# Attention, routing and two feed-forward layers on one core: scores by bank, casts placed around GpSimd, squares moved to the expert stage

## The chip, the cores and the metric

The kernel runs on one core of a Trainium2 chip. TensorE (PE) multiplies, VectorE (DVE), ScalarE (ACT) and GpSimd (POOL) work on elements, SyncE (SP) and queues of the other engines start transfers. The metric is the time of the device for one launch, the median of three runs; lower is better.

## The reference

Four batches of eight heads with 576 rows of 64 go through a causal attention with a decay; its output is a table of 2304 tokens of 512. Each token is routed to one of eight experts by the cosine with the experts' embeddings, and scaled by its gate. A second layer, common to all tokens, follows.

```python
scores = scale * np.matmul(q, k.transpose(0, 1, 3, 2))
decay = cum[:, :, :, None] - cum[:, :, None, :]          # cum: running sum of log f
scores = np.where(causal, -1e9, scores + decay)          # softmax over the last axis, times v
xn = x / (norm(x) + 1e-06);  en = expert_emb / (norm(expert_emb) + 1e-06)
logits = xn @ en.T / tau;    expert_idx = argmax(logits) # gate_w: softmax's value there
out[mask] = gate_w[mask, None] * (np.maximum(x[mask] @ w1[e], 0) @ w2[e])      # for each e
h = np.maximum(np.maximum(x @ w1, x @ w2), x @ w3);  return h @ w_out
```

The norm of a token scales all its logits alike, so the choice of the expert doesn't need it; the gate does. The sums of squares of the tokens' rows are therefore wanted late, when the gates are worked out.

## The kernel before

Attention runs over 32 heads in 16 pairs. A head's 576 rows are five blocks t of 64, 128, 128, 128 and 128 rows that see 64, 192, 320, 448 and 576 columns. Products are made from numbers split in a high part and a rest: for each pair `split_tasks` casts q to `At` (`q_hi`) and k to `R1` (`k_hi`), on VectorE or ScalarE, and GpSimd subtracts to get the rests (`q_lo`, L321, and `k_lo`, L324). `q_lo` reads q and its cast, `k_lo` reads k and its cast. In the trace casts and evictions stand on L433 (VectorE) or L435 (ScalarE), the lines of the helper `evict`.

A score tile is one bank of `ps_s` (three banks): `s_task` writes it with two products, `At` by `R` over 128 rows and `Bt` by `R` over 66 (L344), no narrower than 192 columns. Block t = 4 takes two tiles of 288 columns, so a head has six tiles, in the order t = 4, 0, 3, 1, 2. `r_task` reduces each on VectorE (L361: scale, mask and row minimum in one instruction, written to `P`, and a read of the accumulator to `nm`), which frees the bank; ScalarE's exponential follows (L381). `P` is turned by transposes on TensorE into banks of `ps_t` (two named t, L397 and L401, one named tl for the last 64 columns of each block, L393 and L399), which are evicted to `PT`. `pair_out` multiplies with v (`po`, L459), evicts to `ot`, turns back with the logits beside it (`pb`, L478), divides by the sums (L445, L446) and writes `XL` (L487) and x to memory.

After the last pair of a batch `batch_out` starts two chains: `route_batch`, which ranks the batch's tokens by expert and adds them to a table of rows (VectorE steps and a few products), and `square_sums`, five ScalarE squares (L703). Batch 3's routing is followed by the gathers for the experts.

The expert stage computes for each of eight experts, with 384 to 256 tokens, eight tiles `ph` and from them `h`, then four tiles `py` into `Y`; weights come through the ring `stg` on SP's queue and are cast to `w` (L934) with a subtraction behind; tokens come through gathers, a transpose (`xt`) and a cast to `x` (L934). The part of `Y` beyond the first expert's columns is cleared once (L1103). `side_work` works out norms and gates beside it. The shared layer follows from about 500 us.

All of this is put in order by a list scheduler, `Sched`: a task has engines with costs, a priority and predecessors, and the plan takes at each step the task that can start first, of these the one with the lowest priority number. The instructions are issued in the plan's order on each engine; a predecessor that only the plan knows makes no wait on the chip. There an instruction waits for the data, buffers and registers that it uses and for those ahead of it on its engine.

Of the kernel before, what the change touches and what calls it, by code (L numbers as in the profile page):

```python
# [12 lines left out]
ALU = mybir.AluOpType  # L13
# [201 lines left out]
def attention(tc, g, qT, kT, v, x_dram, es):  # L215
# [132 lines left out]

    def r_task(h, t, k, j0, w, n, ext):
        def fn(e):  # L350
            if k == 0:
                if t == order[0] and h % H == 0:
                    b = h // H
# [6 lines left out]
            m0 = S - 128 if t == 0 else S - ext + j0  # L360
            nc.vector.tensor_tensor_reduce(out=P[0:n, j0:j0 + w], in0=st_.pop((h, t, k))[0:n, 0:w], in1=g.mask[0:n, m0:m0 + w],  # L361
                                           scale=-0.125, scalar=(3.0e38 if k == 0 else nm[0:n, 0:1]),
                                           op0=ALU.add, op1=ALU.min, accum_out=nm[0:n, k:k + 1])

        deps = [fs[h, t, k]] + ([fr[h, t]] if k else [])
        fr[h, t] = sd.task("DVE", dve(w), fn, slot[h, t], deps, get=None if k else ("P", (h, t)), rel=[("s", (h, t, k))])

    def head(h):
        p, r = divmod(h, 2)
        b = h // H  # L370
        T = PT[h % NPT]
# [14 lines left out]
        for t in order:  # L386
# [20 lines left out]
            if t == 0:  # L407
                continue
# [1051 lines left out]
```

## Time and profile before

| what | us |
|---|---|
| median of three runs | 785.85 (785.13 to 787.29) |
| the profiled execution | 785.06 |
| its span, first to last instruction | 783.3 |
| TensorE busy | 738.9 (94%) |
| VectorE, ScalarE, GpSimd busy | 461.9, 368.2, 237.7 |

The profile is of one execution. Its stages, by the trace: attention from about 15 to 222 us, the routing of batch 3 with the first gathers to 238, experts to about 500, the shared layer to the end. A line of a group names engine, operation, output and inputs with their sizes and the number of instructions. A timeline's line gives the start, the duration and, in brackets, how long the engine had nothing to do and what it waited for. Matmuls overlap: from one start to the next is what one costs.

### The profile page before, as it was taken

How to read it: one execution, taken by the hardware profiler on the slowest of the kernel's cores; microseconds unless marked ns; L12 is line 12 of the kernel's file. 1: busy time of each engine (PE TensorE's matmuls, PEld its weight loads, DVE VectorE, ACT ScalarE, POOL GpSimd, SP SyncE). 2: the span in 40 equal slices, each digit the busy share in tenths (PEclk: the TensorE clock that was granted, in tenths of full speed). 3: DMA queues.
4: the chain of work that ended last, by engine and by line, in shares of the span. 5: the costliest groups of instructions: out<-in, count | busy, mean ns of one | idle time of the engine just before them, and what ended most of it. 6: DMA issues, size and time to landing. Idle time of an engine off the chain costs nothing.

```text
span 783.3 us, 13403 instructions
## 1 busy us (share of the span) xinstructions
PE 738.9 (94%) x4862; PEld 682.3 (87%) x4862; DVE 461.9 (59%) x1076; ACT 368.2 (47%) x870; POOL 237.7 (30%) x189
## 2 busy tenths in 40 slices
PE   2989999999949998999999999999999999999996
PEld 1868877778738998999999999989999899999995
DVE  6888887988567998867767877941211211112110
ACT  5668887978836653454554563231211212212111
POOL 7464443532020344234223113341221211212112
PEclk9999999999978999999999999999999999999998
DMA  9959775751145465556474653200000000100001
GB/s 228 239 125 216 191 178 143 182 118 40 23 116 208 151 220 181 186 181 233 151 257 147 230 198 126 82 28 14 1 40 1 28 14 1 41 0 15 28 1 43
DMA packets 44614, 90.19 MB, mean 115 GB/s; under 512 B 23320, under 2 KB 23320, under 8 KB 44544
## 3 DMA queue, kind: packets, MB, share of 16 engines
q1 hardware_dynamic: 40960, 77.83, 34.0%
q0 software_dynamic: 3152, 9.88, 3.5%
q10 hardware_dynamic: 432, 1.57, 0.5%
q8 instruction: 40, 0.66, 0.3%
q14 instruction: 30, 0.25, 0.1%
HBM read 74.97 MB, written 9.44 MB: 108 GB/s over the span
## 4 chain that ended last, share of the span: by engine, by line
PE 75%; DVE 9%; DMA 7%; issue 4%; ACT 1%; POOL 1%; SPq 1%; POOLq 0%; DVEq 0%; ACTq 0%
PE pm L907 10%; PE pm L906 10%; PE pm L908 10%; PE s L344 6%; PE po L459 6%; PE t L397 4%; PE ph L908 3%; PE ph L907 3%; PE py L906 3%; PE py L908 3%; PE ph L906 3%; PE py L907 3%; PE po L1268 3%; PE po L1267 3%; PE po L1266 3%
## 5 line engine op out<-in xcount | busy, mean ns | idle before, releaser
L1240 DVE TENSOR_TENSOR tm<-pm,tm 128x384 f32<-128x384 f32 x72 | 40.1, 557 | 199.4 <-PE pm L908 198.2
L907 PE MATMUL pm<-x_y,m 128*128 128x384 f32 x432 | 144.5, 335 | 0.0
L908 PE MATMUL pm<-x_y,m 128*128 128x384 f32 x432 | 144.4, 334 | 0.0
L906 PE MATMUL pm<-x_y,m 128*128 128x384 f32 x432 | 144.4, 334 | 0.0
L381 ACT ACTIVATE P<-P,nm 128x576 f32<-128x576 f32 (+4 forms) x160 | 88.3, 555 | 17.0 <-DVE nm L361 16.7
L344 PE MATMUL s<-R,At 128*128 128x192 f32 (+1 forms) x192 | 71.3, 380 | 14.9 <-DVE At L271 10.5
L934 ACT ACTIVATE w<-stg 128x1024 fp32r<-128x1024 f32 x63 | 66.2, 1056 | 33.3 <-DMA stg<-in_w_dram 14.4
L907 PEld LDWEIGHTS pm<-x_y,m 128*128 128x128 f32 x432 | 81.1, 188 | 0.6 <-POOL x_y L1199 0.3
L951 DVE TENSOR_TENSOR w<-stg,w 128x1024 fp32r<-128x1024 f32 x54 | 70.2, 1304 | 19.3 <-ACT w L934 18.9
L907 PE MATMUL ph<-x,w 128*128 128x384 f32 (+7 forms) x256 | 79.3, 310 | 2.1 <-DVE x L1083 2.1
L906 PEld LDWEIGHTS pm<-x_y,m 128*128 128x128 f32 x432 | 81.1, 188 | 0.2
L908 PEld LDWEIGHTS pm<-x_y,m 128*128 128x128 f32 x432 | 81.1, 188 | 0.0
L906 PE MATMUL py<-h,w 128*128 128x384 f32 (+7 forms) x256 | 79.5, 311 | 0.8 <-DVE h L1141 0.8
L908 PE MATMUL ph<-x,w 128*128 128x384 f32 (+7 forms) x256 | 79.4, 310 | 0.8 <-DVE w L951 0.7
L906 PE MATMUL ph<-x,w 128*128 128x384 f32 (+7 forms) x256 | 79.4, 310 | 0.7 <-ACT x L934 0.7
L1251 POOL TENSOR_TENSOR g<-tm,g 128x384 fp32r<-128x384 f32 x34 | 36.5, 1074 | 141.4 <-ACT g L934 141.4
L908 PE MATMUL py<-h,w 128*128 128x384 f32 (+7 forms) x256 | 78.5, 307 | 0.4 <-DVE w L951 0.4
L907 PE MATMUL py<-h,w 128*128 128x384 f32 (+7 forms) x256 | 78.2, 305 | 0.0
L934 ACT ACTIVATE g<-tm 128x384 fp32r<-128x384 f32 x36 | 18.8, 524 | 115.9 <-DVE tm L1240 115.9
L361 DVE CUSTOM_DVE_ANT_0 P<-s,mask 128x288 f32<-128x288 f32 (+4 forms) x160 | 64.4, 422 | 11.1 <-PE s L344 6.7
L344 PE MATMUL s<-R,Bt 66*128 66x192 f32 (+1 forms) x192 | 60.2, 320 | 4.3 <-DMA R<-clo 4.3
L321 POOL TENSOR_TENSOR At<-q,At 64x1152 fp32r<-64x1152 f32 x15 | 40.3, 2684 | 77.1 <-DVE At L433 24.7
(246 smaller groups left out, 1620.4 us busy)
## 6 DMA issues: line engine op xcount, KB each, us to landing
stg<-in_w_dram SPq DMA_DIRECT2D x61, 512.0 KB
q<-in_q_dram SPq DMA_DIRECT2D x32, 288.0 KB
k<-in_k_dram SPq DMA_DIRECT2D x32, 288.0 KB
sd<-in_m_dram SPq DMA_DIRECT2D x18, 512.0 KB
Bt<-At SPq DMA_DIRECT2D x16, 288.0 KB
v<-in_v_dram SPq DMA_DIRECT2D x4, 1024.0 KB
x_dram<-XL SPq DMA_DIRECT2D x64, 64.0 KB
sd_o<-in_mo_dram SPq DMA_DIRECT2D x6, 512.0 KB
```

Of the source, the lines that this page charges most:

```text
L321: nc.gpsimd.tensor_tensor(out=At[i][64:128], in0=raws[p][0][64:128], in1=At[i][64:128].bitcast(F32), op=ALU.subtract)
L344: nc.tensor.matmul(st[:, 0:wp], lt[0:kk, r, ROW0[t]:ROW0[t] + 128], rt[0:kk, r, j0:j0 + wp], start=(ps_i == 0), stop=(ps_i == 1))
L361: nc.vector.tensor_tensor_reduce(out=P[0:n, j0:j0 + w], in0=st_.pop((h, t, k))[0:n, 0:w], in1=g.mask[0:n, m0:m0 + w], scale=-0.125, scalar ...
L381: nc.scalar.activation(out=P[0:n, 0:ext], in_=P[0:n, 0:ext], func=AF.Exp, bias=nm[0:n, k:k + 1], scale=-1.0, accum_out=sums[b][0:n, t, h % ...
L459: nc.tensor.matmul(po[64 * r:64 * r + 64, lo - c0:w], vt[b][0:n, a, (2 * hp + r) * D:(2 * hp + r + 1) * D], PT[(2 * p + r) % NPT][0:n, a, ...
L906: nc.tensor.matmul(out, whi, xhi, start=start, stop=False)
L907: nc.tensor.matmul(out, whi, xlo, start=False, stop=False)
L908: nc.tensor.matmul(out, wlo, xhi, start=False, stop=stop)
L934: nc.scalar.activation(out=out, in_=in_, func=AF.Copy)
L951: ENG[e].tensor_tensor(out=w[:, 1], in0=t, in1=w[:, 0].bitcast(F32), op=ALU.subtract)
L1240: nc.vector.tensor_tensor(out=mx[0], in0=mx["p", w][:, 0:MC], in1=mx[0], op=ALU.max)
L1251: ENG[e].tensor_tensor(out=ht[:, 1, :], in0=mx[0], in1=ht[:, 0, :].bitcast(F32), op=ALU.subtract)
```

## The change

Casts. The costs in the plan become 1.1 (ScalarE) and 0.8 us (VectorE), 2.7 us for a subtraction. Both casts of a pair get the pair before's `k_lo` as a predecessor, `q_lo` gets both casts and `k_lo` gets `q_lo`. The instructions and what they read are the same.

```diff
-        qh = sd.task(("ACT", "DVE"), (1.02, 0.67), q_hi, u, old + [load])
-        ql = sd.task("Pool", 2.6, q_lo, u, [qh])
+        qh = sd.task(("ACT", "DVE"), (1.1, 0.8), q_hi, u, old + [load, quiet[0]])
         qc = sd.task("SP", 0.9, q_copy, u, [qh], lat=2.0)
-        kh = sd.task(("ACT", "DVE"), (1.02, 0.67), k_hi, u, old + [load])
-        kl = sd.task("Pool", 2.6, k_lo, u, [kh])
+        kh = sd.task(("ACT", "DVE"), (1.1, 0.8), k_hi, u, old + [load, quiet[0]])
+        ql = sd.task("Pool", 2.7, q_lo, u, [qh, kh])
+        kl = quiet[0] = sd.task("Pool", 2.7, k_lo, u, [kh, ql])
```

Scores. Six tiles of a head become four units, one bank each: the halves of t = 4, t = 2 with t = 1, and t = 3 with t = 0, whose product is now 64 columns wide. The reductions of a shared bank go in the reverse order, and the last one frees it.

```diff
+    UNITS = (((4, 0, 0, 288, 0),), ((4, 1, 288, 288, 0),), ((2, 0, 0, 320, 0), (1, 0, 0, 192, 320)), ((3, 0, 0, 448, 0), (0, 0, 0, 64, 448)))
+    FLIPS = ((4,), (2, 1), (3, 0))
...
+    def s_unit(h, n):
...
+        u = slot(h, n)
+
+        def mm(e):
+            st = st_[h, n] = ps_s.tile([128, 512], F32, tag="s", name=f"s_{h}_{n}")
+            for t, k, j0, w, c in UNITS[n]:
+                for ps_i, (lt, rt, kk) in enumerate(((At[i], R1[i], 128), (Bt[i], R2[i], 66))):
+                    nc.tensor.matmul(st[:, c:c + w], lt[0:kk, r, ROW0[t]:ROW0[t] + 128], rt[0:kk, r, j0:j0 + w],
+                                     start=(ps_i == 0), stop=(ps_i == 1))
+
+        cost = 0.08 + sum(2 * max(0.112, 0.013 + x[3] / 2400) for x in UNITS[n])
+        dep = fs[h, n] = sd.task("PE", cost, mm, u - LEAD, ready[p], get=("s", (h, n)))
+        for x, (t, k, j0, w, c) in enumerate(UNITS[n][::-1]):
+            def red(e, t=t, k=k, j0=j0, w=w, c=c):
+                if n == 0 and h % H == 0:
                     sums[b] = sm.tile([128, NBLK, H], F32, tag="sums", name=f"sums{b}", bufs=2)
                     nc.vector.memset(sums[b][64:128, 0, :], 1.0)
-                P = pp.tile([128, S], F32, tag="P", name=f"P_{h}_{t}")
-                nm = sm.tile([128, 2], F32, tag="nm", name=f"nm_{h}_{t}")
-                Pt[h, t] = P, nm
-            P, nm = Pt[h, t]
...
+                if k == 0:
...
+                nc.vector.tensor_tensor_reduce(out=P[0:m, j0:j0 + w], in0=st_[h, n][0:m, c:c + w], in1=g.mask[0:m, m0:m0 + w],
+                                               scale=-0.125, scalar=(3.0e38 if k == 0 else nm[0:m, 0:1]),
+                                               op0=ALU.add, op1=ALU.min, accum_out=nm[0:m, k:k + 1])
...
+            end = x == len(UNITS[n]) - 1
+            dep = fr[h, t] = sd.task("DVE", dve(w), red, u, [dep] + ([fr[h, t]] if k else []), get=None if k else ("P", (h, t)),
+                                     rel=[("s", (h, n))] if end else [])
...
+                fe[h, t] = sd.task("ACT", 0.28 + EXT[t] / 1200, exp, u, [fr[h, t]])
+
+    def slot(h, n):
+        return 5 * h + (0, 0.5, 1.5, 3)[n]
```

Transposes. Three groups t = 4, t = 2 with 1, and t = 3 with 0 take the place of four; the tl bank is taken at a head's start.

```diff
+        def tail(t, P):
+            nc.tensor.transpose(tl_[h][0:64, 128 * t - 128:128 * t], P[:, 128 * t:128 * t + 64], g.ident)
+
+        def start(e):
+            tl_[h] = ps_t.tile([128, 512], F32, tag="tl", name=f"tl_{h}", bufs=1)
+            tail(4, Pt[h, 4][0])
...
+        u4 = slot(h, 0) + LT
+        ft[h, "tl"] = sd.task("PE", 0.06, start, u4, [fe[h, 4]], get=("tl", h))
...
+            def tr(e, ts=ts):
+                w = tl_[h, ts] = ps_t.tile([128, 512], F32, tag="t", name=f"t_{h}_{ts[0]}")
+                c = 0
+                for t in ts:
+                    P = Pt.pop((h, t))[0]
+                    for a in range(t):
+                        nc.tensor.transpose(w[:, c:c + 128], P[:, 128 * a:128 * a + 128], g.ident)
+                        c += 128
+                    if t == 0:
+                        nc.tensor.transpose(w[0:64, c:c + 64], P[0:64, 0:64], g.ident[0:64, 0:64])
+                    elif t != 4:
+                        tail(t, P)
+
...
+            ft[h, n] = sd.task("PE", cost, tr, u + LT, [fe[h, t] for t in ts] + [ft[h, "tl"]], get=("t", (h, n)),
+                               rel=[("P", (h, t)) for t in ts])
...
-        fv[h, 0] = sd.task(("ACT", "DVE"), (act(256), dve(256)), tail, slot[h, order[-1]] + LT - 4,
-                           [ft[h, t] for t in order] + old, rel=[("tl", h)])
+        fv[h, "tl"] = sd.task(("ACT", "DVE"), (act(256), dve(256)), corners, slot(h, 3) + LT - 4,
+                              [ft[h, n] for n in range(len(FLIPS))] + old, rel=[("tl", h)])
```

Routing and squares. Batches 0 to 2 only reduce their logits when they end; one routing handles fifteen blocks after batch 2. The squares of these batches leave attention. In the expert stage, SP reads x again into the unused part of `Y`, ScalarE squares it there, and only then is that part cleared; `side_work` comes after these squares.

```diff
-        sd.chain(g.square_sums(b, lambda: XL[b][:, :, :, 0:D]), pr + 40, deps + [consts_done])
+        if b == B - 1:
+            sd.chain(g.square_sums(b, lambda: XL[b][:, :, :, 0:D]), pr + 40, deps + [consts_done])
...
+def logits(nc, g, b, lg):
+    yield dict(eng="DVE", cost=0.75)
+    nc.vector.tensor_reduce(out=g.L[:, NBLK * b:NBLK * b + NBLK, :], in_=lg().rearrange("p t h c -> p t c h"), op=ALU.add, axis=AX.X)
...
+def route_batch(nc, g, b, lg, rp, sp, ps):
+    yield from logits(nc, g, b, lg)
+    if b < B - 2:
+        return
...
+    m, b0 = (1, b) if last else (B - 1, 0)
+    s0, nb = NBLK * b0, NBLK * m
...
+    for c in range(m):
+        yield dict(eng="DVE", cost=0.83)
+        ohp = onehot_pos(nc, g, rm[:, NBLK * c:NBLK * c + NBLK], NBLK, keep, "rb")
+        yield dict(eng="PE", cost=0.2, get=None if c else ("o", ("pt", b)))
+        if c == 0:
+            pt = ps.tile([128, 512], F32, tag="o", name=f"ptab{b}")
+        table_sums(nc, pt, ohp, rr[:, NBLK * c:NBLK * c + NBLK], c == 0, c == m - 1)
+    yield dict(eng="DVE", cost=0.24, rel=[("o", ("pt", b))])
+    table_add(nc, g, pt)
```

```diff
-    sd.chain(side_work(nc, g, g.cp, rp, ps_o), 30.0, [sorted_])
...
-    zero = [sd.task("ACT", 1.8, lambda e, d=d: clear(e, d), now + 16, [wsplit[1, 0, 3]]) for d in range(KC)]
+    room = [Y[d][:, CAP[0]:CAP[0] + 4 * DM].rearrange("p (t d) -> p t d", t=4) for d in range(KC)]
+    xv = x_dram.rearrange("(b n) d -> b n d", n=S)
+
+    def fetch(e, d):
+        if d < B - 1:
+            nc.sync.dma_start(out=room[d], in_=xv[d, 64:S].rearrange("(t p) d -> p t d", p=128))
+        else:
+            nc.sync.dma_start(out=room[d][0:64, 0:B - 1], in_=xv[0:B - 1, 0:64].rearrange("b p d -> p b d"))
+
+    def square(e, d, i):
+        n, col = (128, NBLK * d + 1 + i) if d < B - 1 else (64, NBLK * i)
+        x = room[d][0:n, i]
+        nc.scalar.activation(out=x, in_=x, func=AF.Square, accum_out=g.ss[0:n, col:col + 1])
+
+    zero, norms = [], []
+    for d in range(KC):
+        xl = sd.task("SP", 1.5, lambda e, d=d: fetch(e, d), now + 10 + 5 * d, [wsplit[1, 0, 3]], lat=4.0)
+        mine = [sd.task("ACT", 0.62, lambda e, d=d, i=i: square(e, d, i), now + 18 + 6 * d, [xl]) for i in range(4 if d < B - 1 else B - 1)]
+        zero.append(sd.task("ACT", 1.8, lambda e, d=d: clear(e, d), now + 18 + 6 * d, mine))
+        norms += mine
+    sd.chain(side_work(nc, g, g.cp, rp, ps_o), 50.0, [sorted_] + norms)
```

How the order moves. First VectorE, at the casts of pair 10 (`q_10`, `k_10`): `P` with `nm` is a reduction of a score tile `s_`, named by the block in its first number (before) or by the unit (now), and `ot` an eviction. Before:

```order
L433 CAST At_111<-q_10_1514 128x1152
L361 ISA P_4_1681,nm_4_1682<-s_4_1_1676,mask,nm_4_1682 128x288
L361 ISA nm_4_1682 128x1
L361 ISA P_0_1716,nm_0_1717<-s_0_0_1697,mask 64x64
L361 ISA nm_0_1717 64x1
L361 ISA P_3_1719,nm_3_1720<-s_3_0_1701,mask 128x448
L361 ISA nm_3_1720 128x1
L433 CAST R_117<-k_10_1515 128x1152
L433 COPY ot_0_1730<-po_0_1709 128x320
```

Now:

```order
L447 CAST At_111<-q_10_1465 128x1152
L365 ISA P_1_1617,nm_1_1618<-s_2_1586,mask 128x192
L365 ISA nm_1_1618 128x1
L365 ISA P_2_1627,nm_2_1628<-s_2_1586,mask 128x320
L365 ISA nm_2_1628 128x1
L459 TENSOR_SCALAR rs_1633<-sums_878 128x10
L460 RECIPROCAL rs_1633<-rs_1633 128x10
L447 CAST R_117<-k_10_1466 128x1152
L365 ISA P_0_1659,nm_0_1660<-s_3_1638,mask 64x64
```

Before, three reductions (the second half of t = 4, t = 0 and t = 3) stood between the two casts; now the reductions of t = 1 and t = 2, from one bank, and the two instructions on the sums stand there.

TensorE in a head of the same stretch, from the transposes of t = 4 (before) and of t = 2 (now) on; `s_` are the score products, `t_` and `tl` the transposes. Before:

```order
L397 MATMUL t_4_1606<-ident,P_4_1494 128x128 x4
L478 MATMUL pb_1_1617<-w_223,ot_1_1599 128x144 x2
L344 MATMUL s_0_0_1627<-R_117,At_111 128x192
L344 MATMUL s_0_0_1627<-R_120,Bt_114 128x192
L393 MATMUL tl_1630<-ident,P_4_1494 64x128
L344 MATMUL s_3_0_1633<-R_117,At_111 128x448
L344 MATMUL s_3_0_1633<-R_120,Bt_114 128x448
L397 MATMUL t_3_1640<-ident,P_3_1543 128x128 x3
L399 MATMUL tl_1630<-ident,P_3_1543 64x128
L344 MATMUL s_1_0_1649<-R_117,At_111 128x192
L344 MATMUL s_1_0_1649<-R_120,Bt_114 128x192
L397 MATMUL t_1_1652<-ident,P_1_1560 128x128
```

Now:

```order
L409 MATMUL t_2_1544<-ident,P_2_1449 128x128 x2
L392 MATMUL tl_1515<-ident,P_2_1449 64x128
L409 MATMUL t_2_1544<-ident,P_1_1439 128x128
L392 MATMUL tl_1515<-ident,P_1_1439 64x128
L349 MATMUL s_3_1554<-R_117,At_111 128x448
L349 MATMUL s_3_1554<-R_120,Bt_114 128x448
L349 MATMUL s_3_1554<-R_117,At_111 128x64
L349 MATMUL s_3_1554<-R_120,Bt_114 128x64
L409 MATMUL t_3_1564<-ident,P_3_1484 128x128 x3
L392 MATMUL tl_1515<-ident,P_3_1484 64x128
L412 MATMUL t_3_1564<-ident,P_0_1481 64x64
L349 MATMUL s_0_1577<-R_118,At_112 128x288
```

The 192-wide product of t = 0 has become a 64-wide one behind t = 3 in the same bank, and the transposes of two blocks follow each other.

ScalarE in the first expert, from `h_5` on; `w_0_3` is the last quarter of the first expert's second weight, `x_1` the second expert's tokens, L1164 a square and L1150 or L1103 a clear. Before:

```order
L1135 ACTIVATE h_5_3687<-ph_5_3645 128x384
L1103 ACTIVATE Y_3421<-ident 128x1920
L1135 ACTIVATE h_6_3711<-ph_6_3670 128x384
L1103 ACTIVATE Y_3422<-ident 128x1920
L1103 ACTIVATE Y_3423<-ident 128x1920
L1135 ACTIVATE h_7_3750<-ph_7_3691 128x384
L934 ACTIVATE w_0_2_3762<-stg_0_2_3705 128x1024
L934 ACTIVATE w_0_3_3795<-stg_0_3_3744 128x1024
L934 ACTIVATE w_1_0_3835<-stg_1_0_3784 128x1024
L934 ACTIVATE x_1_3849<-xt_0_3837 128x4x128
```

Now:

```order
L1202 ACTIVATE h_6_3498<-ph_6_3467 128x384
L982 ACTIVATE w_0_1_3500<-stg_0_1_3463 128x1024
L1164 ACTIVATE Y_3241,ss<-Y_3241 128x512
L1202 ACTIVATE h_7_3514<-ph_7_3485 128x384
L1164 ACTIVATE Y_3241,ss<-Y_3241 128x512 x3
L1150 ACTIVATE Y_3241<-ident 128x1920
L1164 ACTIVATE Y_3242,ss<-Y_3242 128x512 x4
L1150 ACTIVATE Y_3242<-ident 128x1920
L982 ACTIVATE w_0_3_3602<-stg_0_3_3554 128x1024
L1164 ACTIVATE Y_3243,ss<-Y_3243 128x512 x2
L982 ACTIVATE x_1_3636<-xt_0_3614 128x4x128
L982 ACTIVATE x_1_3636<-xt_1_3620 128x4x128
```

The clears have moved behind `h_7` and between them and it stand the squares; the cast of `w_0_3` comes after eight squares and two clears, the casts to `x_1` after ten.

## Rows read from the trace of the kernel before

**Rows 1.** The page's busy totals: busy us, share of the span, instructions.

```profile
PE 738.9 (94%) x4862; PEld 682.3 (87%) x4862; DVE 461.9 (59%) x1076; ACT 368.2 (47%) x870; POOL 237.7 (30%) x189
```

**Rows 2.** Stretches: length, then busy us of PE, PEld, DVE, ACT, POOL; PEclk, DMA share, GB/s.

```profile
60.00:200.00 140.00, 136.61 (x1132) 111.49 (x1131) 118.97 (x430) 117.83 (x383) 55.71 (x21) 1.00 0.63 148
```

**Rows 3.** Waits of PE, 60 to 200 us: total, times, longest.

```profile
PE pb L478 <- DVE ot L433: 1.7, 2, 0.9
PE s L344 <- DVE nm L361: 1.7, 2, 0.8
```

**Rows 4.** Timeline of PE, 47.4 to 47.9 us: start, us, idle before it.

```profile
47.60 0.46 PE L344 MATMUL s<-R,At 128*128 128x192 f32 x1 [2.38 <-DVE nm L361]
```

**Rows 5.** Stretches, the long wait and what follows it.

```profile
44.00:48.00 4.00, 1.62 (x13) 1.41 (x12) 3.92 (x7) 1.02 (x3) 3.25 (x2) 0.96 0.17 38
48.00:52.00 4.00, 4.00 (x22) 3.27 (x21) 2.24 (x10) 2.48 (x10) 3.92 (x2) 0.61 1.01 250
```

**Rows 6.** Timeline of VectorE, 38 to 47.7 us.

```profile
43.51 2.63 DVE L433 CAST At<-q 128x1152 fp32r<-128x1152 f32 x1
```

**Rows 7.** Timeline of GpSimd, 38 to 47.7 us.

```profile
42.89 2.63 POOL L324 TENSOR_TENSOR R<-k,R 64x1152 fp32r<-64x1152 f32 x1 [0.75 <-DVE R L433]
```

**Rows 8.** Timeline of VectorE, 100.5 to 105.2 us.

```profile
100.82 0.76 DVE L433 CAST At<-q 128x1152 fp32r<-128x1152 f32 x1
...
101.89 3.07 DVE L433 CAST R<-k 128x1152 fp32r<-128x1152 f32 x1
```

**Rows 9.** Timeline of GpSimd, 100.5 to 105.2 us.

```profile
101.71 2.64 POOL L321 TENSOR_TENSOR At<-q,At 64x1152 fp32r<-64x1152 f32 x1 [2.42 <-DVE At L433]
```

**Rows 10.** Groups by form, casts and subtraction: busy us, mean ns.

```profile
L321 POOL TENSOR_TENSOR At<-q,At 64x1152 fp32r<-64x1152 f32 x15 | 40.3, 2684 | 77.1 <-DVE At L433 24.7 <-ACT At L435 21.1 <-DMA R<-clo 6.8
...
L433 DVE CAST R<-k 128x1152 fp32r<-128x1152 f32 x13 | 26.5, 2036 | 0.0
```

**Rows 11.** Timeline of PE, 193.1 to 195.2 us.

```profile
193.58 0.25 PE L344 MATMUL s<-R,At 128*128 128x192 f32 x1
193.67 0.28 PE L344 MATMUL s<-R,Bt 66*128 66x192 f32 x1
193.78 0.38 PE L397 MATMUL t<-ident,P 128*128 128x128 f32 x2
194.00 0.27 PE L399 MATMUL tl<-ident,P 128*64 128x128 f32 x1
194.03 0.39 PE L344 MATMUL s<-R,At 128*128 128x320 f32 x1
```

**Rows 12.** Groups by form, reductions of the last bank.

```profile
L361 DVE CUSTOM_DVE_ANT_0 P<-s,mask 128x448 f32<-128x448 f32 x32 | 19.7, 615 | 2.7 <-PE s L344 1.3 <-ACT P L381 0.6
...
L361 DVE CUSTOM_DVE_ANT_0 P<-s,mask 64x64 f32<-64x64 f32 x32 | 6.7, 209 | 0.0
```

**Rows 13.** Groups by form, squares and clears.

```profile
L703 ACT ACTIVATE sq<-XL 128x512 f32<-128x512 f32 x20 | 12.5, 624 | 1.3 <-DVE XL L487 1.1
...
L1103 ACT ACTIVATE Y<-ident 128x1920 f32<-128x1920 f32 x4 | 7.1, 1801 | 0.0
...
L703 ACT ACTIVATION_READ_ACCUMULATOR sq<-XL 128x1 f32 x20 | 3.8, 192 | 0.0
```

**Rows 14.** Timeline of ScalarE, 256 to 272 us.

```profile
258.78 0.48 ACT L1135 ACTIVATE h<-ph 128x384 fp32r<-128x384 f32 x1
259.14 3.16 ACT L934 ACTIVATE w<-stg 128x1024 fp32r<-128x1024 f32 x3
```

**Rows 15.** Timeline of PE, 258 to 259 us.

```profile
257.75 0.33 PE L908 MATMUL py<-h,w 128*128 128x384 f32 x1
257.93 0.33 PE L906 MATMUL py<-h,w 128*128 128x384 f32 x1
```

**Rows 16.** Waits of PE, 236 to 330 us.

```profile
PE ph L906 <- ACT x L934: 0.7, 1, 0.7
```

**Rows 17.** Stretches, the first expert.

```profile
238.00:260.00 22.00, 21.96 (x114) 21.56 (x115) 16.68 (x44) 18.06 (x21) 0.42 (x1) 0.90 0.56 200
```

More of the change, by code (lines that the diff above doesn't have):

```diff
@@ L307, in split_tasks @@
         if p > 1:
-            old = [fs[h, t, k] for h in (2 * p - 6, 2 * p - 5) for t in range(NBLK) for k in range(1 + (t == 4))] if p >= NQ else []
+            old = [fs[h, n] for h in (2 * p - 6, 2 * p - 5) for n in range(4)] if p >= NQ else []
             load = sd.task("SP", 3.3, lambda e: load_pair(p), u - 8, ready[p - 2], lat=2.0)
@@ L349, in r_task @@
[L349 to L353, printed above, removed]
+        b, i = h // H, p % NQ
+        u = slot(h, n)
[5 more added lines that the diff above has]
+                                     start=(ps_i == 0), stop=(ps_i == 1))
@@ L420, in tail @@
-        def tail(e):
+        for n in range(4):
+            s_unit(h, n)
+        old = [fo[p - 2, u] for u in range(2)] if p >= 2 else []
+        def tail(t, P):
[5 more added lines that the diff above has]
+        ft[h, "tl"] = sd.task("PE", 0.06, start, u4, [fe[h, 4]], get=("tl", h))
@@ L446, in recip @@
             nc.vector.reciprocal(rs[0], rs[0])
-        rt = sd.task("DVE", 0.35, recip, u0, [fe[h, t] for h in hs for t in order])
+        rt = sd.task("DVE", 0.35, recip, u0, [fe[h, t] for h in hs for t in range(NBLK)])
         for u, (c0, w) in enumerate(RNG):
@@ L590, in route_batch @@
                                    op1=ALU.is_equal)
-    yield dict(eng="PE", cost=0.2, get=("o", ("pr", b)))
+    yield dict(eng="PE", cost=0.05 * (nb + 1), get=("o", ("pr", b)))
     pr = ps.tile([128, 512], F32, tag="o", name=f"pr{b}")
-    w = NBLK * E
+    w = nb * E
     fl = oh.rearrange("p t e -> p (t e)")
     nc.tensor.matmul(pr[:, 0:w], g.tris, fl, start=True, stop=False)
-    if b:
+    if b0:
         nc.tensor.matmul(pr[:, 0:w].rearrange("p (t e) -> p t e", e=E), g.ones,
                          g.ohs.unsqueeze(1).to_broadcast(SH), start=False, stop=False)
-    for d in range(1, NBLK):
-        nc.tensor.matmul(pr[:, d * E:w], g.ones, fl[:, 0:w - d * E], start=False, stop=(d == NBLK - 1))
+    for d in range(1, nb):
+        nc.tensor.matmul(pr[:, d * E:w], g.ones, fl[:, 0:w - d * E], start=False, stop=(d == nb - 1))
     if last:
@@ L603, in route_batch @@
         return
-    yield dict(eng="DVE", cost=0.24, rel=[("o", ("pr", b))])
-    r1 = rp.tile(SH, F32, tag="r1", name="r1")
+    yield dict(eng="DVE", cost=0.3, rel=[("o", ("pr", b))])
     nc.vector.tensor_tensor(out=r1, in0=pr[:, 0:w].rearrange("p (t e) -> p t e", e=E), in1=oh, op=ALU.mult)
@@ L677, in first_slot, with row_ids, table_sums, table_add @@
     g.rest = ohp, rc
[L680 to L689 removed]
+def row_ids(nc, g, oh, b0, m, rc, rr):
+    nb = NBLK * m
+    SC, SR = [128, nb, NCH], [128, nb, E, NCH]
+    yield dict(eng="DVE", cost=0.24)
+    idv = g.idv[:, b0:b0 + m, :].rearrange("p b t -> p (b t)")
+    nc.vector.tensor_tensor(out=rc, in0=rc, in1=idv.unsqueeze(2).to_broadcast(SC), op=ALU.mult)
+    yield dict(eng="DVE", cost=0.28 * m)
+    nc.vector.tensor_tensor(out=rr, in0=oh.unsqueeze(3).to_broadcast(SR), in1=rc.unsqueeze(2).to_broadcast(SR), op=ALU.mult)
+def table_sums(nc, pt, ohp, rr, first, last):
+    for t in range(NBLK):
+        nc.tensor.matmul(pt[:, 0:E * NCH], ohp[:, t, :], rr[:, t].rearrange("p e c -> p (e c)"),
+                         start=(first and t == 0), stop=(last and t == NBLK - 1))
+def table_add(nc, g, pt):
+    nc.vector.tensor_tensor(out=g.tab, in0=g.tab, in1=pt[:, 0:E * NCH].rearrange("p (e c) -> p e c", c=NCH), op=ALU.add)
+def route_table(nc, g, b, ohp, rc, rp, ps):
+    oh = g.oh[:, NBLK * b:NBLK * b + NBLK, :]
+    rr = rp.tile([128, NBLK, E, NCH], F16, tag="rr", name="rr")
+    yield from row_ids(nc, g, oh, b, 1, rc, rr)
     yield dict(eng="PE", cost=0.2, get=("o", ("pt", b)))
     pt = ps.tile([128, 512], F32, tag="o", name=f"ptab{b}")
[L692 to L694 removed]
+    table_sums(nc, pt, ohp, rr, True, True)
     yield dict(eng="DVE", cost=0.24, rel=[("o", ("pt", b))])
[L696 removed]
+    table_add(nc, g, pt)
 def square_sums(nc, g, b, x, rp):
```

139 lines of the change are left out of this document (49 added, 90 removed).

## The prediction

> **What bounds the kernel now.** I read the busy totals first: TensorE is busy for 94% of the span, VectorE for 59%, ScalarE for 47%, GpSimd for 30% [rows 1]. The table by stretches then says that this holds inside attention too, the stage that the change touches most: between 60 and 200 us TensorE works for 136.61 of 140.00 us at a full granted clock, VectorE for 118.97 [rows 2]. So work that is taken from VectorE or ScalarE is worth nothing by itself; only what TensorE waits for can pay. The list of TensorE's waits in that stretch has two rows of two waits, 3.4 us in all: an output product that waits for the eviction of `ot` by VectorE, and a score product that waits for a reduction to free its bank [rows 3].
>
> One wait is much larger and lies earlier: the score product at 47.60 us starts after 2.38 us without work, and again a reduction is what it waited for [rows 4]. The granted clock was 0.96 in the four microseconds of that wait and 0.61 in the next four, with TensorE busy all the time [rows 5]; its work there was worth 0.61 x 4.00 = 2.44 us at full clock, so 1.56 us went with the clock. The wait and its echo cost 3.9 us.
>
> Behind the wait stands a cast. On VectorE the cast of q at 43.51 us takes 2.63 us [rows 6] beside a subtraction of GpSimd that runs from 42.89 to 45.52 [rows 7]. The collision is clearer at 101 us: the first cast takes 0.76, the second starts at 101.89, takes 3.07 and ends at 104.96 [rows 8]; GpSimd's subtraction runs from 101.71 to 104.35 [rows 9]. The 13 casts of k on VectorE take 2.036 us in the mean against 0.76 for a cast that meets nothing, beside subtractions of 2.684 [rows 10]. 13 x (2.04 - 0.76) = 16.6 us of VectorE are lost so, and nearly all of it costs TensorE nothing, because score banks are in store.
>
> The Trainium skill says of this, in "SBUF — State Buffer", section "Who interferes with whom", that VectorE's fast modes and GpSimd contend for one lock, and that whoever issues first keeps it for its whole instruction. The trace agrees (the cast ends 0.6 us after the subtraction), and by that rule a cast escapes only if it is issued before the subtraction.
>
> **The change part by part.** *Casts between the subtractions.* The plan now puts both casts ahead of the first subtraction. Its data, though, are as they were: the subtraction of q reads q and its cast, not the cast of k, so GpSimd may start it as soon as the first cast ends. In the new VectorE order of pair 10 two reductions and the reciprocals still stand between the two casts. I therefore expect the cast of k to be blocked in most pairs as now, and to end about 3.3 us after the first cast; what stands between is simply done in that time. What does change is the clump at 38 to 47 us, where the cast of k of one pair and the cast of q of the next each met a subtraction: the casts of a pair are now behind the last subtraction of the pair before, and pair 3's cast of k is on ScalarE. I count the wait and its echo as gone, -3.9 (0 if another clump takes its place).
>
> *Score products by bank, and where evictions go.* The twelve score products, six reductions and five exponentials of a head stay; six bank uses become four, and fifteen transposes go through three banks in place of four. Two reductions in a row now hold one bank. Of the 32 evictions of `ot` VectorE had seven and now has three, so the two `ot` waits, 1.7 us, should go; of the two waits for a reduction I take half, -0.8. Sum -2.5. Bounds: -3.4, all four gone; and +5, if two reductions per bank make the blocked casts show in the ten pairs with work between them, 10 x 0.8 us, the length of the short waits for a reduction, less the 3.4 that are there now.
>
> *The narrower product.* Only t = 0 changes, from 192 to 64 columns, 32 times. Now the pair of 192-wide products takes 193.58 to 193.78, 0.20 us [rows 11]. The spacing of wide ones follows their columns; by that a 64-wide pair would take 0.08, a gain of 32 x 0.12 = 3.8. The nearest rows say otherwise: two transposes that move 128 columns take 0.22 together, 0.11 each, and the one that moves 128 columns over a stationary tile of half the width is done in 0.03 [rows 11]. A floor of 0.11 set by the stationary tile gives 2 x 0.11, +0.02 x 32 = +0.6. Between -3.8 and +0.6 I take 0, next to the transposes.
>
> The Trainium skill, "TensorE: Matmul & The Clock Gate", section "LDWEIGHTS (loading the stationary operand)", lets the load go by the columns of the stationary operand. The 0.11 and 0.03 agree; by that rule the narrowing would be worth nothing, by the columns moved -3.8.
>
> *Pair 2.* Its two casts now stand side by side at about 28 us, the second fully blocked: 2.3 us (3.07 - 0.76) of VectorE early, when few scores are in store. +0.5 (0 to 2.4).
>
> *The last head* ends with the bank of t = 3 and t = 0, whose reductions take 0.209 + 0.615 [rows 12], in place of t = 2 with 320 columns (0.615 x 320 / 448 = 0.44 by its columns): 0.4 more before the last exponential, and its eviction is larger: +0.5 (-0.5 to +1).
>
> *Routing of three batches at once.* VectorE loses about thirty instructions, some 6 us by their durations of 0.2 to 0.8; TensorE does as many products. Cover: TensorE bounds that stretch. 0. The routing of batch 3, between attention and experts, is as before.
>
> *Squares in the expert stage.* Fifteen squares at 0.624 + 0.192 us, 12.2 us of ScalarE, leave attention [rows 13], where TensorE is the bound: 0. They come back in the first expert, with 3.5 MB of transfers, and four clears of 1.80 us [rows 13] now wait for them. ScalarE goes through its row in order: between the last `h` and the cast of w2's last quarter stand seven squares and two clears. Seven squares 5.7, two clears 3.6, the `h` itself 0.48 and the cast, 1.05 (3.16 for three) [rows 14], make 10.8 us from the start of the second product; the subtraction behind it, taken at the length of a cast, 11.9. TensorE needs that quarter after three others of 24 products at 0.173 us [rows 15], 12.5. The margin is 0.6 us, and the tokens of expert 1, next in ScalarE's row, have as little. Today ScalarE holds up the tokens' product once, for 0.7 us [rows 16]. DMA moves 200 GB/s there at a share of 0.56 [rows 17], so 357 at full share and 157 to spare, an estimate. I take +1.5: twice the 0.7 us wait. Bounds: -3.5, if VectorE, rid of waits, closes the short waits of that stage, and +8.5, below.
>
> Sum: -3.9 - 2.5 + 0 + 0.5 + 0.5 + 0 + 1.5 = -3.9. The profiled execution took 785.06 us (span 783.3), so 781.16; it is 0.79 below the median shown, so **782.0**.
>
> **Rivals.** *The casts collide as before.* The order is a plan; the lock is not asked by it. For it: the second cast still starts behind the start of the subtraction; against it: the clump has no twin in the new order. Half of the 3.9 is then gone, the short waits stay: -2.0 + 0.5 + 0.5 + 1.5 = +0.5, so 786.4.
>
> *More is gained.* All waits of attention go, and the narrow product goes by its columns: -3.9 - 3.4 - 3.8 + 0.5 = -10.6, so 775.2. For it: wide products do follow their columns; against it: the transposes' 0.11.
>
> *ScalarE's squares hold up the first expert.* If the rows of x for the second set of squares arrive behind weights, ScalarE stands at that square and the cast of w2's quarter and the tokens of expert 1 stand behind it. The two fetches in front, 2.1 MB, take 5.9 us at the full 357 GB/s and 13.4 at the 157 to spare; 7.5 us late, less the margin of 0.6, is 6.9, and such a wait brings the clock's echo, 1.6 as above: 8.5 in place of 1.5, so 789.0, slower. It decides from a delay of 0.6 us on and makes the kernel slower from 6 us on. For it: no slack in ScalarE's row; against it: DMA is half idle there, and the fetches are issued ahead of the quarter they must not delay.
>
> **How the numbers follow.** The forecast has 0.46, with a range of its own from 779 to 785; colliding casts 0.22; more gain 0.13; the first expert 0.19. About 0.3% is what a measurement of this kernel tells from no change: 2.4 us, 783.5 and 788.2. Faster: the forecast without its upper edge, 0.42, and more gain, 0.13, 0.55. Slower: most of the first expert's case, 0.16, and the upper part of the colliding casts, 0.04, 0.20. The rest, 0.25, is within 0.3%. The range goes from 774, under the rival that gains more, to 791, over the first expert's: 1.5 to 2 in 10 lie outside, most of them where several costs at the +5 and +8.5 bounds meet.
>
> **What would show it.** Right: no wait over 1 us between 30 and 60 us and a granted clock near 1 there; waits of TensorE from 60 to 200 us under 2 us, none for `ot`; casts of k still near 2 us in the mean; ScalarE's squares between 245 and 285 us without a wait of TensorE over 1 us. Wrong: a score product that waits over 0.5 us in every other pair (casts), start spacings of 64-wide products near 0.04 us (narrowing), or waits of the expert products for a cast of ScalarE or for weights in the first two experts.

## The result: slower by 1.1%

The changed kernel takes 794.9 us (median of four, 791.78 to 797.19) against 785.49 beside it; the ratio is 1.0113, 95% interval 1.0073 to 1.0153. The forecast was 782.0 in a range of 774 to 791: the direction was wrong and the time lies outside the range.

Where the time went, from first and last instructions of each stage in the two traces:

| stage | before | changed | difference |
|---|---|---|---|
| attention, first score to last `pb` | 210.86 | 208.82 | -2.0 |
| routing of batch 3, first gathers | 16.49 | 16.94 | +0.4 |
| experts, first `ph` to first `pm` | 239.16 | 251.39 | +12.2 |
| shared layer and end | 306.25 | 306.26 | 0 |

Attention first. The stretches that answer to [rows 2] and [rows 5], columns as there:

```profile
44.00:48.00 4.00, 4.00 (x33) 3.92 (x33) 4.00 (x20) 4.00 (x15) 2.46 (x1) 1.00 0.90 193
48.00:52.00 4.00, 4.00 (x36) 3.36 (x35) 3.59 (x10) 3.43 (x14) 2.11 (x1) 1.00 0.31 63
60.00:200.00 140.00, 136.81 (x1125) 112.30 (x1124) 119.30 (x401) 105.53 (x359) 56.76 (x22) 1.00 0.63 148
```

The long wait and its clock echo are gone: TensorE is busy for all of 44 to 52 us at full clock. But from 60 to 200 us it stands still nearly as long as before (3.19 us against 3.39). TensorE's waits from 14 to 222 us of the changed kernel, total, times, longest:

```profile
PE s L349 <- DMA R<-clo: 4.6, 1, 4.6
PE pr L624 <- DVE oh L618: 2.5, 1, 2.5
PE pb L492 <- ACT ot L449: 2.3, 4, 0.7
PE tl L392 <- DVE nm L365: 1.6, 1, 1.6
PE s L349 <- DVE nm L365: 1.0, 1, 1.0
```

The `ot` waits did not go, they went from VectorE to ScalarE [rows 3]. The casts are blocked as the prediction said, a little more than before [rows 10]:

```profile
L447 DVE CAST R<-k 128x1152 fp32r<-128x1152 f32 x13 | 31.2, 2397 | 0.2 <-DMA k<-in_k_dram 0.2
L447 DVE CAST At<-q 128x1152 fp32r<-128x1152 f32 x13 | 9.9, 762 | 0.0
```

Now the experts. TensorE's waits from 238 to 490 us (the same list of before, from 238 to 490, comes to 4.7 us with 1.7 as the longest):

```profile
PE py L954 <- DVE h L1208: 3.9, 1, 3.9
PE ph L955 <- DVE x L1131: 2.1, 2, 1.3
PE ph L956 <- POOL w L999: 1.9, 1, 1.9
PE py L956 <- DVE w L999: 1.8, 3, 0.7
PE ctps L907 <- DVE x L1131: 1.6, 1, 1.6
PE ph L956 <- DVE w L999: 0.8, 2, 0.6
PE xt L1120 <- DVE x L1131: 0.2, 1, 0.2
```

Six of the seven name VectorE and none ScalarE, whose row the prediction feared. The fetches and squares cost TensorE nothing where they stand: between 238 and 260 us TensorE is busy throughout, with the DMA share at 0.97 in place of 0.56 [rows 17]:

```profile
238.00:260.00 22.00, 22.00 (x123) 22.00 (x122) 11.36 (x15) 12.61 (x24) 0.00 (x0) 0.95 0.97 313
```

The same line tells what is missing: VectorE's busy time there fell from 16.68 to 11.36 us. The chain of `side_work` (norms, gates, scatter table), which ran from 238.5 to about 295 us, through the first expert and half of the second, now runs from 276.3 to 331, behind the squares, in the second and third. In the first expert GpSimd is nearly idle (0.42 us of 22 before [rows 17], nothing now); in the second and third it subtracts weights. VectorE's timeline in the third expert, start, us:

```profile
327.06 1.37 DVE L895 TENSOR_TENSOR cc<-io,rq 128x90 f16<-128x90 f32 x1
328.46 2.28 DVE L898 TENSOR_TENSOR cc<-cc,valid 128x90 f16<-128x90 f16 x1
330.78 0.63 DVE L901 TENSOR_TENSOR rr<-cc,val 128x450 f16<-128x450 f16 x1
331.32 1.75 DVE L1208 SCALAR_TENSOR_TENSOR h<-ph,h 128x336 fp32r<-128x336 f32 x4
```

GpSimd beside it:

```profile
326.70 1.61 POOL L1078 TENSOR_TENSOR m<-sd,m 128x512 fp32r<-128x512 f32 x1 [2.39 <-ACT m L982]
328.28 2.35 POOL L999 TENSOR_TENSOR w<-stg,w 128x1024 fp32r<-128x1024 f32 x1
```

And TensorE:

```profile
331.88 0.42 PE L954 MATMUL py<-h,w 128*128 128x336 f32 x1 [3.91 <-DVE h L1208]
```

The four `h` stand in VectorE's row behind the scatter table. Its two steps L895 and L898 each end 0.1 us after the subtraction of GpSimd that runs beside them. In the kernel before the same steps took 0.24 to 0.25 us all four times, for instance:

```profile
285.84 0.24 DVE L847 TENSOR_TENSOR cc<-io,rq 128x90 f16<-128x90 f32 x1
286.12 0.25 DVE L850 TENSOR_TENSOR cc<-cc,valid 128x90 f16<-128x90 f16 x1
```

So 3.2 of the 3.9 us of this wait are time in which the two steps stood behind GpSimd (1.37 - 0.24 and 2.28 - 0.25); that share is read from these rows and was not tested apart. The stretches show the echo, as in [rows 5]; from 333 to 335 us the granted clock is 0.50, the lower of its two levels:

```profile
328.00:332.00 4.00, 0.12 (x1) 0.12 (x2) 3.93 (x5) 1.19 (x2) 2.63 (x2) 1.00 0.53 171
332.00:336.00 4.00, 4.00 (x20) 3.77 (x21) 2.89 (x8) 0.74 (x1) 0.00 (x0) 0.57 0.76 270
```

3.9 us of wait and (1 - 0.57) x 4.00 = 1.7 us of clock: the second product of the third expert takes 22.25 us in place of 16.22. The other 6 us are spread over experts 2 and 6 to 8 (+2.6 in the second product of expert 2, less 1.2 gained in its first, then +1.9, +0.5 and +2.6).

### The profile page after: what moved, and what is told of

The parts are those of the page before. It is cut to its first block, busy times and chain, and to the rows that moved or that the text cites. A ratio compares the mean times of both kernels' runs of the same rounds, so it can differ in the third digit from the quotient of the medians.

```text
span 794.0 us, 13305 instructions
## 1 busy us (share of the span) xinstructions
PE 741.5 (93%) x4860; PEld 686.8 (87%) x4860; DVE 462.2 (58%) x1050; ACT 361.2 (45%) x869; POOL 234.6 (30%) x187
## 4 chain that ended last, share of the span: by engine, by line
PE 75%; DVE 10%; DMA 5%; issue 4%; ACT 2%; POOL 1%; SPq 1%; ACTq 1%; POOLq 0%; DVEq 0%
PE pm L955 9%; PE pm L956 9%; PE pm L954 9%; PE s L349 6%; PE po L473 5%; PE t L409 4%; PE ph L956 3%; PE ph L955 3%; PE ph L954 3%; PE py L954 3%; PE py L956 3%; PE py L955 3%; PE po L1335 3%; PE po L1334 3%; PE po L1333 3%
## 5 line engine op out<-in xcount | busy, mean ns | idle before, releaser
L954 PE MATMUL py<-h,w 128*128 128x384 f32 (+7 forms) x256 | 81.1, 317 | 3.9 <-DVE h L1208 3.9
L956 PE MATMUL py<-h,w 128*128 128x384 f32 (+7 forms) x256 | 79.7, 311 | 1.8 <-DVE w L999 1.8
L955 PE MATMUL py<-h,w 128*128 128x384 f32 (+7 forms) x256 | 79.4, 310 | 0.0
L999 DVE TENSOR_TENSOR w<-stg,w 128x1024 fp32r<-128x1024 f32 x52 | 65.1, 1254 | 21.5 <-ACT w L982 20.8
L349 PE MATMUL s<-R,At 128*128 128x288 f32 (+2 forms) x192 | 64.3, 343 | 11.6 <-DVE At L271 10.6
L349 PE MATMUL s<-R,Bt 66*128 66x288 f32 (+2 forms) x192 | 54.1, 318 | 4.6 <-DMA R<-clo 4.6
```

What stands on the lines that cost most here:

```text
L349: nc.tensor.matmul(st[:, c:c + w], lt[0:kk, r, ROW0[t]:ROW0[t] + 128], rt[0:kk, r, j0:j0 + w], start=(ps_i == 0), stop=(ps_i == 1))
L954: nc.tensor.matmul(out, whi, xhi, start=start, stop=False)
L955: nc.tensor.matmul(out, whi, xlo, start=False, stop=False)
L956: nc.tensor.matmul(out, wlo, xhi, start=False, stop=stop)
L999: ENG[e].tensor_tensor(out=w[:, 1], in0=t, in1=w[:, 0].bitcast(F32), op=ALU.subtract)
```

## The experiments

Times are medians; each ratio is to the kernel before, run on the same chip, with its 95% interval. The runs stood on four chips, on which the kernel before took 785.95 to 786.62 us; e1 to e4 shared one. Stage times are of one profiled execution each.

**Undo the expert-stage part.** e1: the changed kernel with squares in attention again and the old clears and early `side_work`.

```diff
-    sd.chain(side_work(nc, g, g.cp, rp, ps_o), 50.0, [sorted_] + norms)
+    sd.chain(side_work(nc, g, g.cp, rp, ps_o), 30.0, [sorted_])
+    zero = [sd.task("ACT", 1.8, lambda e, d=d: clear(e, d), now + 16, [wsplit[1, 0, 3]]) for d in range(KC)]
```

> The changed kernel with its last part undone: the squares of batches 0 to 2 are again in attention, nothing is fetched for them, and the norms, gates and scatter table start early in the first expert as in the kernel before. Scores by bank, casts, transposes and the one routing stay. All theories that put the loss in the expert stage: about 783 us (785.5 less the 2.0 us by which attention ended earlier in the changed kernel's trace, and up to 0.5 more or less); the expert stage takes 239 us from the first ph to the first pm. A theory that puts it in attention: 792 or more.

Measured 779.77, ratio 0.9919 (0.9897 to 0.9940); experts 239.46, attention 204.80. The stage's whole loss goes with this part, and 4.0 us of attention beside it.

**That part alone.** e2: the kernel before, with fetches, squares and late `side_work`.

> The kernel before with the last part of the change alone: squares, fetches and the late start of the norms in the expert stage. Every theory of the expert stage: about 797.5 us (785.5 + 12). If the loss needs attention's parts as well (their state of the queues at the first expert): below 792.

800.78, ratio 1.0188 (1.0165 to 1.0211); experts 252.81. The loss needs nothing of attention's parts.

**Its pieces.** e3: e1 with the fetches, and clears behind them, without squares. e4: e1 with `side_work` late in the plan, nothing fetched.

```diff
+    late = sd.task("ACT", 0.0, lambda e: None, 50.0, [wsplit[1, 0, 3]], lat=20.0)
+    sd.chain(side_work(nc, g, g.cp, rp, ps_o), 50.0, [sorted_, late])
```

> The kernel of e1 with the fetches of x into Y and the clears behind them, but without squares there (they are in attention) and with the norms and the scatter table early. Theory late side work: as e1, 783 us, within 1.5. Rival transfers (3.5 MB more in the first expert hold up weights and tokens): 790 to 795. Rival ScalarE's squares: as e1.

> The kernel of e1, but the norms, gates and scatter table begin only in the second expert (a delay of 20 us in the plan alone, which puts VectorE's row nearly as in the changed kernel). No fetches and no squares in the expert stage. Theory late side work: as the changed kernel, 793 to 796 us, with a wait of TensorE for h on VectorE of 2 to 5 us in the third expert. Rivals transfers and ScalarE's squares: as e1, 783 us.

e3: 789.39, ratio 1.0048 (1.0032 to 1.0065). e4: 791.00, ratio 1.0064 (1.0041 to 1.0086), 11.2 us over e1, with these two waits in the experts ahead of all others:

```profile
PE xt L1123 <- DVE x L1134: 4.9, 1, 4.9
PE py L957 <- DVE h L1193: 3.4, 1, 3.4
```

So a late chain alone can cost as much as the changed kernel lost. It does so only in part in the same places: the second product of the third expert takes 21.71 us, 5.5 more than in e1 (the changed kernel 6.1 more), but the larger loss of e4, 6.5 us, stands in the second product of the second expert, where the changed kernel loses 2.2, and the eighth expert loses nothing. And e3 loses 9.6 with the chain early: my theory was not the whole, and the rival of the transfers stood.

**No transfer, same plan.** e5: e3 with an empty `fetch`, so that its task is in the plan only.

> The kernel of e3 with its plan unchanged (the fetch tasks still take their place in it and the clears come as late as there), but no fetch is issued. Theory order: what e3 lost (789.4 against 779.8) lies in the order that the planner gives to VectorE and the queues once four more tasks stand on SP; this run takes 788 to 790 us. Rival transfers: the 3.5 MB hold up weights and tokens; this run takes 779 to 781 us. In between: both.

790.98 (786.68 to 793.47), as e3, and its profiled execution, the fastest, still has experts of 245.3 us, 5.9 more than e1. Its waits in the experts:

```profile
PE xt L1123 <- DMA gat<-x_dram,gidx: 3.1, 1, 3.1
PE xt L1123 <- DVE x L1134: 2.2, 1, 2.2
PE ph L959 <- DVE w L1002: 1.6, 3, 0.8
PE py L959 <- DVE w L1002: 1.1, 2, 0.7
PE ph L959 <- POOL w L1002: 0.9, 1, 0.9
```

No byte of x was fetched, so the fetches' transfers are not needed for the loss: four tasks and later clears in the plan make it write another order, in which TensorE meets tokens' transposes (`xt`) and weights that are not ready. The median lies 4.3 us over the profiled execution, so a part of the 11 us over e1 stands in no trace.

**Which of the two.** e12: e5 with the early clears. e13: e1 with late clears, no fetch tasks.

> The kernel of e5 with the clears where e1 has them: only the four fetch tasks on SP are left of the change in the expert stage, in the plan alone (nothing is issued). Theory that SP's time in the plan moves the weights and what hangs on them: 787 to 791 us. Theory that the late clears move ScalarE's and with it VectorE's row: as e1, 779 to 781.

> The kernel of e1 with the clears as late in the plan as in e5, and no fetch tasks. The counterpart of e12: the theory of SP's time expects 779 to 781 us here, the theory of the late clears 787 to 791.

e12: 783.15 (781.34 to 785.97), ratio 0.9981 (0.9964 to 0.9998). e13: 780.55 (777.37 to 781.97), ratio 0.9934 (0.9911 to 0.9957). Neither theory held whole: over e1 they lose 3.4 and 0.8 us, the latter within the noise, both together (e5) 11. One place follows the fetch tasks alone: the first product of the eighth expert takes 14.1 to 15.3 us in all six kernels that have them in the plan (the changed one, e2, e3, e5, e12, e14) and 12.5 in all ten without, e4 and e13 among them.

**Early chain in the changed kernel.** e14: all of the part, but `side_work` at 30.0 and behind `sorted_` alone.

> The changed kernel with all of its last part (fetches, squares and late clears in the expert stage) except that the norms, gates and scatter table start as early as in the kernel before. The gates of the tokens of batches 0 to 2 are then worked out from the initial value of the sums of squares, so that part of the computation is left out. Theory that the late start of VectorE's chain makes a loss of its own in the second and third expert: about 788 to 790 us, as e3, with no wait for h over 1.5 us there; the rest of the loss is the order around fetches and clears. Theory that the late start only follows from the order and costs nothing beside it: 793 to 796, as the changed kernel.

792.62 (789.77 to 796.94), ratio 1.0092 (1.0065 to 1.0119). The second product of the third expert is back at 15.75 us and no wait for `h` is left, as expected. That product is what the late chain decides: 21.3 to 22.3 us in the three kernels with a late chain (the changed one, e2, e4), 15.7 to 16.4 in the thirteen others. But the time is 2.3 us less, not 5 to 7, and the intervals of the two ratios overlap: waits for weights came up instead. From 300 to 490 us:

```profile
PE py L956 <- DVE w L999: 3.6, 5, 1.1
PE ph L956 <- DVE w L999: 1.7, 3, 0.8
PE xt L1120 <- DVE x L1131: 1.4, 2, 1.0
PE py L954 <- ACT w L982: 1.1, 2, 0.7
PE ph L956 <- POOL w L999: 0.9, 1, 0.9
```

e14 has the squares in the expert stage and e3 has not; the stage takes 248.10 and 248.70 us, so the squares by themselves show no cost there.

**Attention's 4 us.** e16: e1 without the squares of batches 0 to 2.

> The kernel of e1 without the squares of batches 0 to 2 (their sums stay at the initial value, this part is left out). Theory that taking ScalarE's work out of attention lets the planner put evictions there that come late: 783 to 784 us, attention about 208.8 us as in the changed kernel, 1.3 us longer in the seventh and the eleventh pair. Theory that the changed kernel's attention was slower for another reason (a spread between executions): as e1, 779 to 780.5.

782.51 (779.35 to 784.56), ratio 0.9962 (0.9941 to 0.9983), 2.7 us slower than e1 with 12.2 us less work on ScalarE. Its seventh and eleventh pair take 13.02 and 13.03 us, as in the changed kernel (13.01 both), against 11.69 in e1; and the wait is the same to the tenth:

```profile
PE pb L492 <- ACT ot L449: 2.3, 4, 0.7
```

In the seventh pair of e1 VectorE evicts `ot` while ScalarE does squares. Without squares the plan gives the eviction to ScalarE, behind an exponential that waits for a reduction, which stands behind a blocked cast (89.85 to 92.99 us). In the changed kernel:

```profile
94.36 0.67 ACT L376 ACTIVATE P<-P,nm 128x448 f32<-128x448 f32 x1 [0.70 <-DVE nm L365]
95.03 0.36 ACT L449 ACTIVATE ot<-po 128x256 f32<-128x256 f32 x1
95.44 0.39 PE L492 MATMUL pb<-w,ot 128*128 128x144 f32 x1 [0.72 <-ACT ot L449]
```

The two pairs make 2.7 of the 4.0 us; 0.8 more stand in the last pair (23.48 us in e16 as in the changed kernel, 22.64 in e1).

**Casts, units, routing apart.** e6: e1 with the old rules for the casts. e7: the kernel before with the new rules alone. e8: the kernel before with the one routing alone.

> The kernel of e1 with the plan's rules for the casts as before (old costs, no predecessor from the pair before, the subtraction of q behind its own cast only). Theory that the casts' rules remove the clump at 38 to 48 us: 783 to 784 us (3.9 us more than e1's 779.8), with a wait of 2 us or more for a reduction in attention. Theory that units and transposes by bank did it: as e1, within 1 us.

> The kernel before with the plan's new rules for the casts alone. Theory that they remove the clump: 782 us (786.0 less 3.9). Theory that units did it: 785 to 787 us.

> The kernel before with the one routing for three batches alone (the squares stay in attention, those of batch 2 behind the routing, with which they share a buffer). By the prediction's term, 0: 784 to 787.5 us. If some 6 us less of VectorE's work shortens attention: 780 to 783.

e6: 778.39, ratio 0.9901 (0.9874 to 0.9927). e7: 777.08, ratio 0.9893 (0.9868 to 0.9919). e8: 782.83 (779.72 to 786.15), ratio 0.9963 (0.9943 to 0.9982). The clump goes with either edit, so e6 refutes that only the casts' rules remove it, e7 that only the units do. Units with the routing (e6) gain 8.2, the casts' rules alone (e7) 9.5, all of them 6.2 (e1): the gains are not a sum of parts. e7 does the work of the kernel before in another order, with five casts of k on ScalarE in place of two; its attention is 9.2 us shorter by that.

**The lock on the chip.** e9: e1 with GpSimd's subtraction of k first, so that it cannot start before the second cast. e10: the same on e7.

```diff
-        ql = sd.task("Pool", 2.7, q_lo, u, [qh, kh])
-        kl = quiet[0] = sd.task("Pool", 2.7, k_lo, u, [kh, ql])
+        kl = sd.task("Pool", 2.7, k_lo, u, [qh, kh])
+        ql = quiet[0] = sd.task("Pool", 2.7, q_lo, u, [qh, kl])
```

> The kernel of e1, but GpSimd does the subtraction of k ahead of that of q. Its first instruction of a pair now reads the second cast, so on the chip, not only in the plan, no subtraction runs while that pair's casts do. The casts of k on VectorE: from 2.4 us in the mean to 0.7 to 1.0 (the lock's theory); a cast of k still at 2 us or more would refute it. Time: theory that VectorE's loss is covered by TensorE: as e1, 779 to 780 us; theory that it shows in the waits: 776 to 778.

> The kernel before with the plan's new rules for the casts and, as in e9, GpSimd's subtraction of k ahead of that of q; nothing else of the change. If what e7 gained (9.5 us) and what e9 gained over e1 (3.4 us, all in the first six pairs, where TensorE waits) add up: 773 to 775 us. If both close the same waits: 776 to 777.5.

e9: 776.37, ratio 0.9885 (0.9858 to 0.9913). The casts of k in e1 and in e9:

```profile
L447 DVE CAST R<-k 128x1152 fp32r<-128x1152 f32 x13 | 25.3, 1946 | 0.3 <-DMA k<-in_k_dram 0.3
```

```profile
L447 DVE CAST R<-k 128x1152 fp32r<-128x1152 f32 x13 | 9.5, 728 | 0.7 <-DMA k<-in_k_dram 0.7
```

The mean falls from 1.946 us to 0.728 by which subtraction goes first. Of the 15.8 us that VectorE gets back (13 x 1.218) the kernel shows 3.4, on another chip than e1 and with intervals that still overlap. From the sixth pair to the last each pair takes what it takes in e1 (11.87 us where no wait is); the profiled attention is 3.0 us shorter, 2.2 of them in the fourth and fifth pair, the rest in the first two, which vary as much between kernels. So both of my expectations were half right. TensorE's list of waits from 17 us to the end of attention is empty, where e1 has 2.7 us ahead of the last batch's routing. e10: 776.84, ratio 0.9895 (0.9875 to 0.9916), no better than e7 or e9; its waits for reductions are those of e7 (0.9 us), so the two edits close the same waits. e7, e9 and e10 beat both kernels, by about 1.1 and 2.3%.

## Why the prediction was wrong, point by point

- *Squares in the expert stage, +1.5 with a bound of +8.5*, is the step that failed: +12.2. It was worked out from ScalarE's row, and that row held: the squares ran from 254.6 to 275.3 us and no product waited for the cast of w2's last quarter or for `x` on ScalarE. What it left out, and so put at nothing, is the edit's last line. `side_work` was moved behind the squares, out of an expert in which VectorE had room (16.68 of 22 us busy) and GpSimd was idle, into one in which both are busy (18.55 and 6.42 of 20 us from 320 to 340 us). That makes 6 us of the 12.2, the second product of the third expert, long in every kernel with a late chain and in no other. e4 shows that a late chain alone can cost as much as the whole (11.2 us over e1); e14 shows that it is not necessary, since the fetch tasks and late clears order VectorE's row anew too (e5), which the prediction did not count either: 1.6 us in the eighth expert's first product come with the fetch tasks.
- *The long wait and its echo, -3.9*: right, gone in every kernel with either edit (44 to 52 us above). The prediction gave it to the casts' rules alone; the units do it too (e6).
- *Evictions and banks, -2.5*: wrong. I counted evictions that leave VectorE and did not ask what stands ahead of them on ScalarE. In the changed kernel 2.3 us of waits for `ot` came back there, and TensorE's idle time from 60 to 200 us fell by 0.2 us only; with the squares kept in attention (e1) the waits for `ot` are 0.3.
- *Casts*: the mechanism was right, blocked at 2.4 us in the mean since the data and not the plan release GpSimd. The Trainium skill's rule in "SBUF — State Buffer", section "Who interferes with whom", held also where I turned it round: with issue order forced the other way (e9) the cast takes 0.728 us. That VectorE's loss is covered by TensorE held from the sixth pair on.
- *The narrower product, 0*: a size. The 64-wide pair takes 0.15 us, start to start, in the mean of 32 heads. Against the 0.20 of [rows 11] that is 32 x 0.05 = -1.6 us, an estimate: those rows have a pair that follows another score product, as the 64-wide one always does, while most of the 192-wide pairs before followed transposes or output products and took 0.28 to 0.30, so what width and place did was not taken apart. In the timeline the 64-wide `At` product gives way after 0.03 us and the `Bt` product after 0.11, so the floor of 0.11 that I gave to both held for one:

```profile
195.03 0.20 PE L349 MATMUL s<-R,At 128*128 128x64 f32 x1
195.06 0.28 PE L349 MATMUL s<-R,Bt 66*128 66x64 f32 x1
195.17 0.55 PE L409 MATMUL t<-ident,P 128*128 128x128 f32 x3
```

- *Routing, 0*: -3.1 us in e8, with squares that are also arranged otherwise there; whose part it is was not taken apart. *Pair 2 and the last head, +1.0*: the last pair takes 23.48 us against 21.75 before (22.64 in e1), more than the 0.5; the start was not separated from its spread (the first pair took 14.9 to 16.9 us in kernels with the same rules for the casts).
- The parts of attention came to -5.4 in the sum. The kernel that has them without the last part, e1, shows -6.1 there. That is luck in part: the terms for evictions and for the routing were wrong, and the parts do not add up (e6, e7). Between the two profiled executions the miss is 14.6 us (795.72 against the 781.16 of the sum): 10.7 in the experts' term, 3.4 in attention's terms, 0.4 in the routing.
- The rival on the slower side named the right stage and the wrong engine, and with 0.19 was held too unlikely. The rival that gains more leaves out the squares' 1.5 and one of the two terms of 0.5; with them its sum is -8.6 and not -10.6. It had no part in the miss.

What stays open: which of the exchanges in the order make the rest of the loss, in the changed kernel as in e3, e5 and e14. The waits are mostly for weights and tokens that VectorE prepares, in different experts each time, and taking away one of the causes in the plan moved them.

## What to carry to other kernels

When an edit changes what a task waits for, follow everything that the task releases: here fifteen cheap squares delayed a chain of another engine by 38 us, out of a stretch with room into one without. Ask for each stretch that gets new work which engines are at work there already, and whether they lock each other; the same VectorE steps took 0.25 us beside an idle GpSimd and 1.4 to 2.3 beside a busy one. With a planner that places everything, test parts alone and in pairs: here parts with gains of 8.2 and 9.5 us made 6.2 together, and plan tasks that issue nothing, with later clears, cost 11.

## What the runs showed of the hardware

VectorE steps on 20 elements per partition wait for GpSimd as long as large casts do. The gates' steps in the changed kernel, by line, and GpSimd's three subtractions from 288.30 us beside them, one of which each step waits out:

```profile
L879 DVE TENSOR_SCALAR val<-gr 128x20 f16<-128x20 f32 x1 | 2.3, 2336 | 0.0
L877 DVE TENSOR_TENSOR gr<-gr,val 128x20 f32<-128x20 f32 x1 | 2.3, 2302 | 0.0
L876 DVE CAST val<-gr 128x20 f16<-128x20 f32 x1 | 2.3, 2286 | 0.0
```

```profile
288.30 7.12 POOL L999 TENSOR_TENSOR w<-stg,w 128x1024 fp32r<-128x1024 f32 x3 [18.06 <-DVE gr L873]
```

The same three in the first expert of the kernel before:

```profile
L828 DVE CAST val<-gr 128x20 f16<-128x20 f32 x1 | 0.2, 201 | 0.0
L831 DVE TENSOR_SCALAR val<-gr 128x20 f16<-128x20 f32 x1 | 0.2, 200 | 0.0
...
L829 DVE TENSOR_TENSOR gr<-gr,val 128x20 f32<-128x20 f32 x1 | 0.2, 181 | 0.0
```

With 7.57 MB moved between 238 and 262 us at a share of 0.96, and 4.42 MB in the kernel before, no wait of TensorE for weights or tokens appeared in that stretch.
